# Seven half products in place of eight for the first MoE matrix product, from the third unit on

## The chip, the cores and the metric

The kernel runs on one core of a Trainium2 chip. A core has a matrix engine (PE; its weight loads are shown apart, as PEld), a vector engine (DVE), a scalar engine (ACT), GpSimd (POOL), and SyncE (SP), which here only issues DMAs. The metric is the device time of one execution in microseconds. Three runs of the kernel before gave 729.53 to 730.95 us, with a median of 729.84 us.

## The reference

Local attention with block summaries, and then a two-layer MoE part whose activation is h - tanh(h):

```
k_sum = k.reshape(B, H, nb, 32, D).max(axis=3);  v_sum = v.reshape(B, H, nb, 32, D).mean(axis=3)
scores_l = scale * q @ k^T, kept where |i - j| < 16
scores_s = scale * q @ k_sum^T + log(32)
a = softmax(concat(scores_l, scores_s));  attn = a @ concat(v, v_sum)
x = attn as [3072 tokens, 512]
h = x @ w_in          # 512 -> 2048, the first MoE matrix product
out = (h - tanh(h)) @ w_out
```

B = 4, H = 8, 768 positions, head width 64. Everything is float32. The weights are drawn as float64 numbers, and the kernel turns their words into float32 itself.

## The kernel before

**Units.** The 3072 tokens are cut into eight units of U = 384 tokens (half a batch). For each unit, attention runs head pair by head pair (NP = 4), in slots of the main loop; the MoE part of a unit follows 22 slots later (LAG), one block f of 128 hidden columns per slot, NF = 16 blocks to a unit.

**The first product.** `moe_in(u, f)` makes h transposed: 128 hidden columns by 384 tokens in one PSUM bank (tag pH, two of them). From unit 1 on each float32 operand is split into two float32r parts, high and low, and the product is the sum of high x high, low x high and high x low. With four chunks of 128 along the model width that is 12 matmuls of 384 moving columns, and each of them loads 128 weight columns of its own. The high parts of the weights are `wh`, the low parts are `wl` (they lie in the buffers `wf`), the parts of x are `xh` and `xl`, made by `x_split`. In unit 0 the product runs in full float32 from `wf` and `split_whole` splits the weights on the way.

**The activation and the second product.** `moe_act_small` reads the bank twice (tanh into gt, square into gu) and gu once more, multiplies the two (g, into gv), and `moe_split` splits g into gh and gl. `moe_out(u, f)` then adds three matmuls of 512 columns to each of three banks pY0 to pY2, nine in all for a block. After 16 blocks `store_y` copies the banks out through the buffers `tmp`.

**What sets the order.** All work is first written down as tasks with the buffers that they read and write. `Plan.schedule` then lays them out in one pass with a cost for each kind, and the list that comes out is the program order of every engine and of SP's DMA queue. Ties and priorities go by tables of offsets (BIAS, KB, SL, HALF). A task may have several engines to choose from (`either`). Buffers with one tag form a ring in program order: a new user waits for the last reader of the buffer that it takes over. The ring `wraw` (three buffers of 4 KB per partition) takes the raw weights, later the chunks of k and v from which the block sums of the later batches are made (`sum_chunks`); `tmp` (three) takes weight words, later the output rows.

**Names in the profile.** All instructions are issued through one wrapper, so the profile gives line 68 for each of them; groups are told apart by their tiles. `pH<-xh,wh` is a matmul of the first product, `pY<-wh,gh` one of the second, `pS<-k,q` scores, `pX<-probT,vw` values, `<-ident,...` transposes.

Of the kernel before, what the change touches and what calls it, by code (L numbers as in the profile page):

```python
# [23 lines left out]
RAWB = 3  # L24
# [35 lines left out]
class Engine:  # L60


    def __init__(self, tc, engine):
        self._tc, self._engine = tc, engine

    def __getattr__(self, name):
        op = getattr(self._engine, name)
        return lambda *args, **kwargs: self._tc.keep_in_program_order(op(*args, **kwargs))  # L68
# [7 lines left out]
HELD = {"w shift", "w low", "w sign", "w low part", "w low part 2", "w high part", "w high part 2", "w scale", "normal", "g high", "g low", "g", "cube", "big", "top pre", "sum guard"}  # L76
# [220 lines left out]
def program(  # L297
# [41 lines left out]

    cpool = ctx.enter_context(tc.tile_pool(name="cpool", bufs=1))  # L340
    wk = ctx.enter_context(tc.tile_pool(name="wk", bufs=2))
    pp = ctx.enter_context(tc.tile_pool(name="pp", bufs=1, space=bass.MemoryType.PSUM))

    px_bank = pp.tile([P, 512], F32, name="pX", tag="pX", bufs=1)
    plan = Plan()

    def do(kind, engine, cost, go, r=(), w=()):
        plan.add(kind, {engine: cost}, go, r, w)

    def either(kind, costs, go, r=(), w=()):  # L350
        if len(costs) > 1:
# [34 lines left out]
    def act(n):  # L386
        return 0.12 + n / 1400
# [104 lines left out]
    def convert(i):  # L492
        f = i // 2
        raw, tmp, res = ("raw", i), ("wt", i), ("w", i)
        buf(raw, "wraw", [P, 2 * DM], U32, RAWB)

        def load():
            if i % 2 == 0:
                src = w_in[:, f * P:(f + 1) * P].rearrange("(c p) n -> p c n", p=P)
                sync.dma_start(at(raw).rearrange("p (c n) -> p c n", c=NC), src.bitcast(U32))  # L500
            else:
                sync.dma_start(at(raw), w_out[f * P:(f + 1) * P, :].bitcast(U32))
        dma("w load", load, P * 8 * DM, 1024 if i % 2 == 0 else 4096, w=[(raw, 0), (raw, 1)])
        buf(tmp, "tmp", [P, DM], F32, 3)

        def words():
            x = at(raw).rearrange("p (n two) -> p n two", two=2)
            return x[:, :, 0], x[:, :, 1], at(tmp)

        def scale(e):  # L510

            _, high, w = words()
            copy(e, w, high.bitcast(F32), 2.0 ** -112)

        def shift():
            w = at(tmp).bitcast(U32)
# [47 lines left out]

    top_of = {}
# [544 lines left out]
```

## Time and profile before

| what | value |
|---|---|
| runs | 729.53, 729.84, 730.95 us |
| the profiled execution, its own time | 725.67 us |
| its span, from the first to the last instruction | 723.9 us |
| mean granted TensorE clock | 0.995 |
| busy share of PE, PEld, DVE, ACT, POOL | 97, 81, 35, 61, 40% |
| DMA | 61.02 MB, 84 GB/s over the span |
| start of the last output copy of unit 0 and of unit 7 | 165.0 and 716.6 us |

The profiled execution is 0.6% below the median of the runs; 1.8 us of its time lie around the span. A busy PE isn't PE at its peak, since matmuls overlap and the ends of their rows are modelled; what a matmul costs in a stream is read from the distance of its start from the next one's. A group row gives the count of its instructions, the busy time, the mean of one in ns and the idle time before them. In the chain, the work that ended last is followed back from the end; its pieces in order of time give a start, a length and how many instructions were merged. The last output copy of unit 1 begins at 258.8 us, so the stretch from 258 us on holds the MoE work of units 2 to 7, and attention up to the last unit beside it.

### The profile page before, as it was taken

The page shows a single profiled execution, that of the slowest core. Times are in us where ns is not written, and L with a number is a line of the kernel's source. Part 1 is how long each engine was busy: PE and PEld are TensorE (multiplying, and loading weights), DVE is VectorE, ACT ScalarE, POOL GpSimd, SP SyncE. Part 2 cuts the span into 40 slices and gives each one's busy share as a digit, 9 for nine tenths or more (in the row PEclk, how much of TensorE's full clock was granted, in tenths as well). Part 3 has the DMA queues.
Part 4 walks back from the last instruction along what each step waited for, and adds up shares of the span by engine and source line. Part 5 has one row for each costly group of instructions (what it writes and reads, how often), then busy time and mean ns, then how long its engine had stood idle before and what let it go on. Part 6 is the DMA issues. An engine that isn't in the chain of part 4 may idle for free.

```text
span 723.9 us, 13669 instructions
## 1 busy us (share of the span) xinstructions
PE 702.3 (97%) x4875; PEld 589.4 (81%) x4875; DVE 251.3 (35%) x842; ACT 442.0 (61%) x1341; POOL 289.3 (40%) x391
## 2 busy tenths in 40 slices
PE   5889999999999999999999999999999999999995
PEld 5776555568889889898988889889898898889984
DVE  3459899893322431521322032232222201110000
ACT  4468777767765665666765466557666556545442
POOL 3001223166333463653444447433343524345443
PEclk9999999999999999999999999999999999999998
DMA  8977667734311150241312012113111201000001
GB/s 208 233 205 204 211 209 211 190 114 132 86 44 43 61 149 10 69 105 56 73 37 50 30 44 71 42 38 93 41 45 29 72 30 41 1 30 16 0 1 49
DMA packets 121518, 61.02 MB, mean 84 GB/s; under 512 B 92512, under 2 KB 113248, under 8 KB 121440
## 3 DMA queue, kind: packets, MB, share of 16 engines
q1 hardware_dynamic: 121440, 60.06, 31.2%
q8 instruction: 40, 0.66, 0.4%
q14 instruction: 38, 0.31, 0.1%
HBM read 51.38 MB, written 6.29 MB: 80 GB/s over the span
## 4 chain that ended last, share of the span: by engine, by line
PE 84%; DMA 5%; ACT 3%; SPq 2%; DVE 2%; POOL 2%; issue 1%; POOLq 0%; DVEq 0%
PE pY L68 36%; PE pH L68 35%; PE pS L68 8%; PE pX L68 5%; SPq L68 2%; DMA wraw<-in_moe_w_out_dram 2%; ACT prob L68 1%; DVE tmp L68 1%; POOL wraw L68 1%; DMA wraw<-in_moe_w_in_dram 1%; DMA gl<-in_v_dram 1%; DMA rawk<-in_k_dram 1%; DMA vw<-in_v_dram 1%; DMA vw<-mean 1%; ACT gu L68 1%
## 5 line engine op out<-in xcount | busy, mean ns | idle before, releaser
L68 PE MATMUL pH<-xh,wf 128*128 128x384 f32 x548 | 185.2, 371 | 0.0
L68 POOL TENSOR_TENSOR gl<-gv,gh 128x384 fp32r<-128x384 f32 x110 | 111.7, 1017 | 169.8 <-ACT gh L68 127.4
L68 PE MATMUL pY<-wf,gh 128*128 128x512 f32 x432 | 177.9, 440 | 0.0
L68 PE MATMUL pH<-xh,wh 128*128 128x384 f32 x448 | 152.9, 341 | 0.0
L68 PE MATMUL pH<-xl,wh 128*128 128x384 f32 x448 | 150.8, 337 | 0.0
L68 PE MATMUL pY<-wh,gh 128*128 128x512 f32 x336 | 140.0, 417 | 0.0
L68 ACT ACTIVATE gu<-pH 128x384 f32<-128x384 f32 x128 | 62.7, 490 | 120.3 <-PE pH L68 94.6
L68 PE MATMUL pY<-wh,gl 128*128 128x512 f32 x336 | 132.3, 394 | 0.0
L68 POOL TENSOR_TENSOR gv<-gu,gt 128x384 f32<-128x384 f32 x95 | 97.3, 1024 | 86.2 <-ACT gu L68 55.3
L68 PEld LDWEIGHTS pH<-xh,wf 128*128 128x128 f32 x548 | 102.5, 188 | 21.4 <-issue 2.8
L68 ACT ACTIVATE prob<-prob,stat 128x118 f32<-128x118 f32 x246 | 91.8, 384 | 22.3 <-DVE stat L68 22.0
L68 PEld LDWEIGHTS pY<-wf,gh 128*128 128x128 f32 x432 | 80.5, 189 | 23.5 <-issue 12.1
L68 DVE CUSTOM_DVE_ANT_0 prob<-pS,mask 128x118 f32<-128x118 f32 x180 | 41.1, 275 | 149.3 <-PE pS L68 125.6
L68 PEld LDWEIGHTS pH<-xh,wh 128*128 128x128 f32 x448 | 84.2, 188 | 3.9 <-issue 0.6
L68 PEld LDWEIGHTS pH<-xl,wh 128*128 128x128 f32 x448 | 84.0, 188 | 0.0
L68 PEld LDWEIGHTS pY<-wh,gl 128*128 128x128 f32 x336 | 63.2, 188 | 14.9
L68 PEld LDWEIGHTS pY<-wh,gh 128*128 128x128 f32 x336 | 63.3, 188 | 11.7 <-issue 2.6
L68 ACT ACTIVATE gh<-gv 128x384 fp32r<-128x384 f32 x82 | 43.1, 525 | 44.5 <-PE pY L68 37.0
L68 ACT ACTIVATE gu<-gu 128x384 f32<-128x384 f32 x128 | 66.9, 523 | 0.0
L68 ACT ACTIVATE gt<-pH 128x384 f32<-128x384 f32 x128 | 61.8, 483 | 0.1
L68 DVE CAST gh<-gv 128x384 fp32r<-128x384 f32 x30 | 11.1, 370 | 135.8 <-PE pY L68 107.7
L68 PE MATMUL pS<-k,q 128*64 128x118 f32 x720 | 42.3, 267 | 0.3 <-ACT k L68 0.3
(130 smaller groups left out, 814.2 us busy)
## 6 DMA issues: line engine op xcount, KB each, us to landing
wraw<-in_moe_w_in_dram SPq DMA_DIRECT2D x16, 512.0 KB
wraw<-in_moe_w_out_dram SPq DMA_DIRECT2D x16, 512.0 KB
rawq<-in_q_dram SPq DMA_DIRECT2D x48, 128.0 KB
out_dram<-tmp SPq DMA_DIRECT2D x24, 256.0 KB
rawk<-in_k_dram SPq DMA_DIRECT2D x32, 128.0 KB
vw<-in_v_dram SPq DMA_DIRECT2D x40, 96.0 KB
vw<-in_v_dram SPq DMA_DIRECT2D x48, 64.0 KB
wraw<-in_k_dram SPq DMA_DIRECT2D x16, 192.0 KB
```

Source lines behind the costliest of these rows:

```text
L68: return lambda *args, **kwargs: self._tc.keep_in_program_order(op(*args, **kwargs))
```

## The change

From unit 2 on, two blocks of hidden columns, g and g + 8, are made together (`moe_in_seven`, g = 0 to 7). The product of the two blocks (256 hidden columns) with the unit (512 by 384) is taken as a two by two product of halves: halves of the model width (256) and halves of the tokens (UH = 192). In place of its eight half products seven are made, with sums of quarters of the operands (the scheme of Strassen and Winograd).

- A half product is 6 matmuls (two chunks, three parts) of 192 moving columns, so a pair has 42 matmuls of 192 columns where it had 24 of 384.
- The four sums of weight quarters are made once, in unit 1, from the split weights (`make_sums`), split into high and low again, and stored to device memory: 16 stores of 512 KB. For each pair they come back in two loads of 512 KB into `wraw` (`load_sums`), 96 loads in all.
- x of a unit is kept whole (`x whole`) and `x_operands` makes four differences of its quarters (8 instructions of 192 columns), and the high and low parts of seven operands.
- The seven products accumulate in two banks of pH, z and y. z is read out four times and y three (`part` and `join`, 192 columns each), through a buffer `s3` into gu. tanh and square then read gu in SBUF, not the bank.
- Room is made for this: `tmp` has two buffers (three before), gu three (two before), the chunks of k and v go through `tmp`, q and k of attention have one buffer from unit 2 on (two before), and the operands of x have one each. The first halves of the weights of blocks 8 to 15 (`wa`) are given up after unit 1.
- In `split_whole` the weights of blocks 8 to 15 are split in two halves each. The tables of the planner are replaced, and so the order of the tasks changes everywhere.

The diff, without the tables and the second program for large values:

```diff
...
-    if not small_only:
+    if small_only:
+        RINGS |= {"gu": 3}
+    else:
         RINGS |= {"gt": 1, "gq": 1}
+    TMPS = 2 if small_only else 3
+    FH, UH, DH = NF // 2, U // 2, DM // 2
+    def seven(u):
+        return small_only and u >= 2
+    def in_halves(i):
+        return small_only and i % 2 == 0 and i // 2 >= FH
...
-            fixed(("wh", i), [P, DM], F32R)
+            if in_halves(i):
+                buf(("wa", i), f"wa{i // 2 - FH}", [P, DH], F32R)
+                fixed(("wb", i), [P, DH], F32R)
+            else:
+                fixed(("wh", i), [P, DM], F32R)
...
-        buf(tmp, "tmp", [P, DM], F32, 3)
+        buf(tmp, "tmp", [P, DM], F32, TMPS)
...
+        x, low = ("wf", i), buf(("wl", i), f"wf{n - 1}" if n else "wl", [P, DM], F32R)
+        parts = [(0, ("wa", i), slice(0, DH)), (1, ("wb", i), slice(DH, DM))] if in_halves(i) else [(0, ("wh", i), slice(0, DM))]
+        for k, high, cs in parts:
+            m = cs.stop - cs.start
+            either("w high part 2", {ACT: act(m) + 0.04, DVE: dve(m, True)}, lambda e, high=high, cs=cs: copy(e, at(high), at(x)[:, cs]), r=[(x, 0)], w=[(high, 0)])
+            do("w low part 2", DVE, dve(m), lambda high=high, cs=cs: vector.tensor_tensor(at(low)[:, cs], at(x)[:, cs], at(high).bitcast(F32), op=ALU.subtract), r=[(x, 0), (high, 0)], w=[(low, k)])
...
+    def w_high(i, c):
+        if in_halves(i):
+            return at(("wb" if c >= NC // 2 else "wa", i))[:, P * (c % (NC // 2)):P * (c % (NC // 2) + 1)]
+        return w_parts(i)[0][:, P * c:P * (c + 1)]
...
+    SCR = ("scr",)
+    if small_only:
+        spool = ctx.enter_context(tc.tile_pool(name="spool", bufs=1, space=bass.MemoryType.DRAM))
+        made[SCR] = spool.tile([FH, 2, P, 4 * DH], F32, name="scr")
+    def make_sums(g):
+        ia, ib = 2 * g, 2 * (g + FH)
+        t0, t1, sf = buf(("tw", g, 0), "tmp", [P, DM], F32, TMPS), buf(("tw", g, 1), "tmp", [P, DM], F32, TMPS), buf(("sf", g), "wraw", [P, 4, DH], F32, RAWB)
+        def add(kind, n, out, x, y, op, r, w):
+            either(kind, {DVE: dve(n), POOL: pool(n)}, lambda e: e.tensor_tensor(out(), x(), y(), op=op), r=r, w=w)
+        add("s whole", DM, lambda: at(t0), lambda: w_parts(ia)[0].bitcast(F32), lambda: w_parts(ia)[1].bitcast(F32), ALU.add, w_keys(ia), [(t0, 0)])
+        for k, n in enumerate(("wa", "wb")):
+            cs = slice(DH * k, DH * (k + 1))
+            add("s whole", DH, lambda cs=cs: at(t1)[:, cs], lambda n=n: at((n, ib)).bitcast(F32), lambda cs=cs: at(("wl", ib))[:, cs].bitcast(F32), ALU.add, [((n, ib), 0), (("wl", ib), k)], [(t1, k)])
+        a11, a12, a21, a22 = (lambda t=t, k=k: at(t)[:, DH * k:DH * (k + 1)] for t in (t0, t1) for k in range(2))
+        s1, s2, s3, s4 = (lambda n=n: at(sf)[:, n] for n in range(4))
+        add("s mix", DH, s1, a21, a22, ALU.add, [(t1, 0), (t1, 1)], [(sf, 0)])
+        add("s mix", DH, s2, s1, a11, ALU.subtract, [(sf, 0), (t0, 0)], [(sf, 1)])
+        add("s mix", DH, s3, a11, a21, ALU.subtract, [(t0, 0), (t1, 0)], [(sf, 2)])
+        add("s mix", DH, s4, a12, s2, ALU.subtract, [(t0, 0), (sf, 1)], [(sf, 3)])
+        for h in range(2):
+            st = buf(("so", g, h), "wraw", [P, 2, 2, DH], F32R, RAWB)
+            keys = [(sf, 2 * h), (sf, 2 * h + 1)]
+            either("s high", {ACT: act(DM), DVE: dve(DM, True)}, lambda e, st=st, h=h: copy(e, at(st)[:, :, 0], at(sf)[:, 2 * h:2 * h + 2]), r=keys, w=[(st, 0)])
+            either("s low", {DVE: dve(DM), POOL: pool(DM)}, lambda e, st=st, h=h: e.tensor_tensor(at(st)[:, :, 1], at(sf)[:, 2 * h:2 * h + 2], at(st)[:, :, 0].bitcast(F32), op=ALU.subtract), r=keys + [(st, 0)], w=[(st, 1)])
+            dma("s store", lambda st=st, h=h: sync.dma_start(made[SCR][g, h], at(st).rearrange("p a b c -> p (a b c)").bitcast(F32)), P * 16 * DH, 4096, r=[(st, 0), (st, 1)], w=[(SCR, (g, h))])
+    def load_sums(u, g, h):
+        st = buf(("sx", u, g, h), "wraw", [P, 2, 2, DH], F32R, RAWB)
+        dma("s load", lambda: sync.dma_start(at(st).rearrange("p a b c -> p (a b c)").bitcast(F32), made[SCR][g, h]), P * 16 * DH, 4096, r=[(SCR, (g, h))], w=[(st, 0)])
...
-            st = buf(("ch", which, b, g, c), "wraw", [P, 8, D], F32, RAWB)
+            st = buf(("ch", which, b, g, c), "tmp", [P, 8, D], F32, TMPS) if small_only else buf(("ch", which, b, g, c), "wraw", [P, 8, D], F32, RAWB)
...
+    def qk_of(u, p):
+        return 0 if seven(u) else p % 2
...
-        qf, kf = ("qf", p % 2), ("kf", p % 2)
+        qf, kf = ("qf", qk_of(u, p)), ("kf", qk_of(u, p))
...
+        if u == 0 and WHOLE_IN or seven(u):
+            if not small_only:
+                buf(("xf", u, p), f"xh{p}", [P, U], F32, 2)
+            elif p == 0:
+                buf(("xf", u), "xf", [P, NC, U])
+            key = (("xf", u), p) if small_only else (("xf", u, p), 0)
+            either("x whole", {ACT: 0.371, DVE: 0.465}, lambda e: copy(e, x_whole(u, p), at(px)[:, :U]), r=[(px, i) for i in range(NT)], w=[key])
...
+        if small_only:
+            buf(xh, f"o{p}", [P, U], F32R)
+            buf(xl, f"o{NC + p}", [P, U], F32R)
...
+    def x_operands(u):
+        xf, tags = ("xf", u), iter(range(12))
+        def part(c, h):
+            return at(xf)[:, c, UH * h:UH * (h + 1)]
+        T = {}
+        for n in range(4):
+            for j in range(2):
+                T[n, j] = buf(("T", u, n, j), f"wa{2 * n + j}", [P, UH])
+        mixes = [(0, lambda j: part(j, 1), lambda j: part(j, 0), lambda j: [(xf, j)]),
+                 (1, lambda j: part(2 + j, 1), lambda j: at(T[0, j]), lambda j: [(xf, 2 + j), (T[0, j], 0)]),
+                 (2, lambda j: part(2 + j, 1), lambda j: part(j, 1), lambda j: [(xf, 2 + j), (xf, j)]),
+                 (3, lambda j: part(2 + j, 0), lambda j: at(T[1, j]), lambda j: [(xf, 2 + j), (T[1, j], 0)])]
+        for n, x, y, keys in mixes:
+            for j in range(2):
+                either("x mix", {DVE: dve(UH), POOL: pool(UH)}, lambda e, n=n, j=j, x=x, y=y: e.tensor_tensor(at(T[n, j]), x(j), y(j), op=ALU.subtract), r=keys(j), w=[(T[n, j], 0)])
+        for name in ("B11", "B21", "T2", "T1", "T3", "T4", "B22"):
+            high, low = (name, u, 0), (name, u, 1)
+            if name == "B22":
+                both = buf((name, u), "q1", [P, 2, 2, UH], F32R)
+                made_by[high], made_by[low] = lambda: at(both)[:, 0], lambda: at(both)[:, 1]
+                hk, lk = (both, "h"), (both, "l")
+            else:
+                for x in (high, low):
+                    buf(x, f"o{next(tags)}", [P, 2, UH], F32R)
+                hk, lk = (high, "h"), (low, "l")
+            if name[0] == "B":
+                c, h = 2 * (name[1] == "2"), int(name[2]) - 1
+                src = [(lambda c=c, h=h: at(xf)[:, c:c + 2, UH * h:UH * (h + 1)], slice(0, 2), [(xf, c), (xf, c + 1)], 2 * UH)]
+            else:
+                src = [(lambda t=T[int(name[1]) - 1, j]: at(t), j, [(T[int(name[1]) - 1, j], 0)], UH) for j in range(2)]
+            for k, (x, cs, keys, n) in enumerate(src):
+                hkk, lkk = [(hk[0], hk[1] + str(k))], [(lk[0], lk[1] + str(k))]
+                either("x high", {ACT: act(n), DVE: dve(n, True)}, lambda e, x=x, cs=cs, high=high: copy(e, at(high)[:, cs], x()), r=keys, w=hkk)
+                either("x low", {DVE: dve(n), POOL: pool(n)}, lambda e, x=x, cs=cs, high=high, low=low: e.tensor_tensor(at(low)[:, cs], x(), at(high)[:, cs].bitcast(F32), op=ALU.subtract), r=keys + hkk, w=lkk)
+            x_keys[u, name] = [(b, n + str(k)) for b, n in (hk, lk) for k in range(len(src))]
+    x_keys = {}
+    def moe_in_seven(u, g):
+        z, y = bank(("z", u, g), "pH"), bank(("yx", u, g), "pH")
+        ha, hb = (buf(("gu", u, f), "gu", [P, U], F32, RINGS["gu"]) for f in (g, g + FH))
+        if ("s3",) not in made_by:
+            buf(("s3",), "k1", [P, 3, UH])
+        s3, ia, ib = ("s3",), 2 * g, 2 * (g + FH)
+        def of_w(i, c0):
+            return lambda c: (w_high(i, c0 + c), w_low(i, c0 + c)), [(("wb", i), 0), (("wl", i), 1)] if in_halves(i) else w_keys(i)
+        def of_s(n):
+            st = ("sx", u, g, n // 2)
+            return lambda c: tuple(at(st)[:, n % 2, k, P * c:P * (c + 1)] for k in range(2)), [(st, 0)]
+        def product(w, x, ps, start):
+            w, keys = w
+            def go():
+                o = at(ps)[:, :UH]
+                for c in range(2):
+                    high, low = w(c)
+                    xh, xl = at((x, u, 0))[:, c], at((x, u, 1))[:, c]
+                    tensor.matmul(o, high, xh, start=start and c == 0, stop=False, skip_group_check=not start)
+                    tensor.matmul(o, low, xh, start=False, stop=False, skip_group_check=not start)
+                    tensor.matmul(o, high, xl, start=False, stop=c == 1, skip_group_check=not start)
+            do("in", PE, 0.53, go, r=keys + x_keys[u, x], w=[(ps, 0)])
+        def part(out, key):
+            either("part", {ACT: 0.27, DVE: 0.28}, lambda e: copy(e, out(), at(z)[:, :UH]), r=[(z, 0)], w=[key])
+        def join(out, key, n):
+            do("join", DVE, 0.28, lambda: vector.tensor_tensor(out(), at(y)[:, :UH], at(s3)[:, n], op=ALU.add), r=[(y, 0), (s3, n)], w=[key])
+        product(of_w(ia, 0), "B11", z, True)
+        product(of_w(ia, 2), "B21", y, True)
+        part(lambda: at(s3)[:, 0], (s3, 0))
+        join(lambda: at(ha)[:, :UH], (ha, 0), 0)
+        product(of_s(1), "T2", z, False)
+        part(lambda: at(s3)[:, 1], (s3, 1))
+        product(of_s(0), "T1", y, True)
+        product(of_s(2), "T3", z, False)
+        part(lambda: at(s3)[:, 2], (s3, 2))
+        join(lambda: at(hb)[:, UH:], (hb, 1), 2)
+        product(of_w(ib, 2), "T4", z, False)
+        part(lambda: at(hb)[:, :UH], (hb, 0))
+        product(of_s(3), "B22", y, False)
+        join(lambda: at(ha)[:, UH:], (ha, 1), 1)
...
+        t, sq = buf(("gt", u, f), "gt", [P, U], F32, RINGS["gt"]), ("gu", u, f)
+        if seven(u):
+            h, hk, sk = (lambda: at(sq)), [], [(sq, 0), (sq, 1)]
+        else:
+            buf(sq, "gu", [P, U], F32, RINGS["gu"])
+            h, hk, sk = (lambda: at(("ph", u, f))[:, :U]), [(("ph", u, f), 0)], [(sq, 0)]
         n = NF * u + f
-        do("tanh", ACT, 0.37, lambda: scalar.activation(at(t), at(ph)[:, :U], AF.Tanh, scale=EC), r=[(ph, 0)], w=[(t, 0)])
-        do("square", ACT, 0.47, lambda: scalar.activation(at(sq), at(ph)[:, :U], AF.Square, accum_out=sums_seen[:, n:n + 1]), r=[(ph, 0)], w=[(sq, 0), (SEEN, n)])
-        do("series", ACT, 0.42, lambda: scalar.activation(at(sq), at(sq), AF.Tanh, scale=EA), w=[(sq, 0)])
+        do("tanh", ACT, 0.37, lambda: scalar.activation(at(t), h(), AF.Tanh, scale=EC), r=hk or sk, w=[(t, 0)])
+        do("square", ACT, 0.47, lambda: scalar.activation(at(sq), h(), AF.Square, accum_out=sums_seen[:, n:n + 1]), r=hk, w=sk + [(SEEN, n)])
+        do("series", ACT, 0.42, lambda: scalar.activation(at(sq), at(sq), AF.Tanh, scale=EA), w=sk)
...
+        u, n = divmod(m, NF)
+        return u, n // 2 + FH * (n % 2) if seven(u) else n
...
-            moe_in(*m)
+            if not seven(m[0]):
+                moe_in(*m)
+            elif m[1] < FH:
+                if m[1] == 0:
+                    x_operands(m[0])
+                for h in range(2):
+                    load_sums(*m, h)
+                moe_in_seven(*m)
             moe_act(*m)
+            if small_only and m[0] == 1 and m[1] >= FH:
+                make_sums(m[1] - FH)
...
```

More of the change, by code (lines that the diff above doesn't have):

```diff
@@ L46 @@
-HALF = {'const': (12, 12), 'k load': (29, 38), 'top pre': (16, 16), 'q load': (9, 15), 'top turn': (8, 8), 'q turn': (4, 9), 'top max': (8, 8), 'q high': (8, 18), 'v load': (44, 63), 'k turn': (5, 9), 'k high': (5, 9), 'top put': (6, 11), 'scores': (4, 9), 'min': (24, 54), 'exp': (24, 54), 'sum': (8, 8), 'sum out': (7, 8), 'sum guard': (4, 9), 'inverse': (4, 9), 'normal': (24, 54), 'p turn': (12, 24), 'p out': (12, 24), 'mean turn': (2, 4), 'mean out': (2, 4), 'mean put': (6, 10), 'values': (4, 4), 'w load': (8, 32), 'x whole': (4, 4), 'w scale': (6, 32), 'w shift': (6, 32), 'w low': (6, 32), 'w sign': (6, 32), 'w high part 2': (6, 32), 'w low part 2': (3, 32), 'in': (2, 20), 'square': (2, 19), 'tanh': (2, 19), 'series': (2, 19), 'g': (1, 19), 'out': (1, 51), 'x high': (0, 4), 'x low': (0, 4), 'chunk load': (0, 11), 'chunk max': (0, 4), 'chunk sum': (0, 4), 'y out': (0, 3), 'y store': (0, 3), 'g high': (0, 2), 'g low': (0, 2), 'top high': (0, 0), 'seen': (0, 0), 'seen turn': (0, 0), 'seen max': (0, 0), 'w high part': (3, 26), 'w low part': (3, 26), 'w sign 1': (4, 12), 'w sign 2': (4, 12), 'top low': (1, 2), 'cube': (2, 18), 'big': (2, 17), 'direct': (2, 17), 'pick': (2, 17), 'q low': (0, 2), 'q again': (0, 2), 'k low': (0, 2), 'k again': (0, 2)}
@@ new lines @@
+HALF = {'const': (12, 12), 'k load': (29, 38), 'q load': (9, 15), 'top pre': (16, 16), 'v load': (44, 63), 'top turn': (8, 8), 'top max': (8, 8), 'q turn': (5, 9), 'q high': (10, 18), 'k turn': (5, 9), 'k high': (5, 9), 'top put': (7, 10), 'scores': (5, 9), 'min': (30, 54), 'exp': (30, 54), 'sum': (8, 8), 'sum out': (8, 8), 'sum guard': (5, 9), 'inverse': (5, 9), 'normal': (30, 54), 'p turn': (15, 24), 'p out': (12, 24), 'mean turn': (2, 4), 'mean out': (2, 4), 'mean put': (6, 10), 'values': (4, 4), 'x whole': (4, 4), 'w load': (7, 32), 'w scale': (6, 32), 'w shift': (4, 32), 'w low': (4, 32), 'w sign': (4, 32), 'w high part 2': (4, 40), 'w low part 2': (2, 35), 'in': (2, 18), 'square': (2, 17), 'tanh': (2, 17), 'series': (2, 17), 'g': (2, 16), 'out': (3, 41), 'x high': (0, 4), 'x low': (0, 4), 'g high': (0, 0), 'g low': (0, 0), 'y out': (0, 0), 'y store': (0, 0), 's whole': (0, 0), 's mix': (0, 0), 's high': (0, 0), 's low': (0, 0), 's store': (0, 0), 'chunk load': (0, 0), 'chunk max': (0, 0), 'x mix': (0, 0), 'chunk sum': (0, 0), 'part': (0, 0), 'join': (0, 0), 's load': (0, 0), 'top high': (0, 0), 'seen': (0, 0), 'seen turn': (0, 0), 'seen max': (0, 0), 'w high part': (3, 26), 'w low part': (3, 26), 'w sign 1': (4, 12), 'w sign 2': (4, 12), 'top low': (1, 2), 'cube': (2, 18), 'big': (2, 17), 'direct': (2, 17), 'pick': (2, 17), 'q low': (0, 2), 'q again': (0, 2), 'k low': (0, 2), 'k again': (0, 2)}
@@ L794, in scores_and_values @@
             banks = [bank(("s", u, p, n), tag) for n, tag in enumerate(tags)]
-            r, w, cost = r + score_keys(p), w + [(x, n) for x in banks for n in range(4)], cost + 1.23
+            r, w, cost = r + score_keys(u, p), w + [(x, n) for x in banks for n in range(4)], cost + 1.23
             parts.append(lambda: score(*now))
@@ L842, in transpose_probs, with x_whole @@
         either("p out", {ACT: 0.28, DVE: 0.335}, lambda e: copy(e, at(pt)[:N2], at(t)[:N2, :2 * P].rearrange("p (a f r) -> p a f r", a=2, f=2)), r=[(t, 0)], w=[(pt, 0)])
+    def x_whole(u, c):
+        return at(("xf", u))[:, c] if small_only else at(("xf", u, c))
     def x_split(u, p):
         px = ("px", u, p)
-        if u == 0 and WHOLE_IN:
-            xf = buf(("xf", u), "xh", [P, NC, U], F32, 2) if p == 0 else ("xf", u)
-            either("x whole", {ACT: 0.371, DVE: 0.465}, lambda e: copy(e, at(xf)[:, p], at(px)[:, :U]), r=[(px, i) for i in range(NT)], w=[(xf, p)])
-            return
@@ new lines, in x_split @@
+        xh, xl = ("xh", u, p), ("xl", u, p)
+        if small_only:
+            buf(xh, f"o{p}", [P, U], F32R)
+            buf(xl, f"o{NC + p}", [P, U], F32R)
+        else:
+            buf(xh, f"xh{p}", [P, U], F32R, 2)
+            buf(xl, f"xl{p}", [P, U], F32R, 2)
+        either("x high", {ACT: 0.371, DVE: 0.465}, lambda e: copy(e, at(xh), at(px)[:, :U]), r=[(px, i) for i in range(NT)], w=[(xh, 0)])
+        do("x low", DVE, 0.47, lambda: vector.tensor_tensor(at(xl), at(px)[:, :U], at(xh).bitcast(F32), op=ALU.subtract),
+           r=[(px, i) for i in range(NT)] + [(xh, 0)], w=[(xl, 0)])
@@ L863, in go @@
                 for c in range(NC):
[L864 to L865 removed]
+                    tensor.matmul(at(ph)[:, :U], at(("wf", i))[:, P * c:P * (c + 1)], x_whole(u, c), start=c == 0, stop=c == NC - 1)
+            do("in", PE, 2.65, go, r=[(("wf", i), 0)] + [(("xf", u), c) if small_only else (("xf", u, c), 0) for c in range(NC)], w=[(ph, 0)])
             split_whole(i)
```

59 lines of the change are left out of this document (27 added, 32 removed).

## The prediction, made blind

> **What bounds the kernel now.** I read the page first: the busy shares, the clock, and the chain of work that ended last.
>
> ```profile
> PE 702.3 (97%) x4875; PEld 589.4 (81%) x4875; DVE 251.3 (35%) x842; ACT 442.0 (61%) x1341; POOL 289.3 (40%) x391
> ...
> PEclk9999999999999999999999999999999999999998
> ...
> PE 84%; DMA 5%; ACT 3%; SPq 2%; DVE 2%; POOL 2%; issue 1%; POOLq 0%; DVEq 0%
> ```
>
> The chain is 84% PE at an open clock, and nothing else holds more than 5%. The busy times by stretch (before unit 1's MoE work, during it, and after it, where the change acts) show how much room there is.
>
> ```profile
> core 0: us, PE busy (x) PEld busy (x) DVE busy (x) ACT busy (x) POOL busy (x), PEclk, DMA share, GB/s
> 0.00:165.00 165.00, 150.74 (x1095) 99.36 (x1096) 125.60 (x343) 107.33 (x318) 40.97 (x76) 0.99 0.72 198
> 165.00:258.00 93.00, 93.00 (x729) 83.17 (x728) 30.77 (x125) 62.02 (x202) 40.39 (x59) 1.00 0.28 72
> 258.00:724.00 466.00, 458.54 (x3055) 406.88 (x3053) 94.94 (x374) 272.63 (x823) 207.90 (x258) 1.00 0.18 46
> ```
>
> In the last stretch PE is never idle until the end, DVE is busy a fifth of the time, ACT 59%, POOL 45%, DMA 18%. The waits of the weight loads there are small: of 13 groups, these are the first three.
>
> ```profile
> PEld pX L68 <- issue: 4.2, 14, 0.4
> PEld pY L68 <- issue: 2.0, 13, 0.2
> PEld pX L68 <- ACT k L68: 0.7, 2, 0.4
> ```
>
> They add up to less than 12 us of 466. So the time from unit 2 on is PE's instruction stream, and the change is priced by what its matmuls cost there. Pieces of the chain in order of time give that price without the modelled ends:
>
> ```profile
> 648.40 4.16 PE pH L68 x24
> 653.27 4.17 PE pH L68 x24
> ...
> 705.38 11.18 PE pY L68 x48
> ```
>
> 24 matmuls of the first product, exactly a pair of blocks, take 4.17 us, 0.174 us each; 48 of the second, with 512 columns, take 0.233 us each. Both are 0.453 to 0.455 ns per column, so these streams are bound by the moving columns. With 192 columns that rate gives 0.087 us, and 42 of them 3.65 us.
>
> **The change, part by part.** *The seven products.* Each of the 42 matmuls still brings 128 weight columns of its own, and now has half the columns to hide the load behind. So the question is what a load costs. Its rows by shape:
>
> ```profile
> L68 PEld LDWEIGHTS pH<-xh,wh 128*128 128x128 f32 x448 | 84.2, 188 | 3.9 <-issue 0.6 <-ACT xh L68 0.3
> L68 PEld LDWEIGHTS pY<-k,q 128*64 128x64 f32 x48 | 2.4, 137 | 0.4 <-POOL k L68 0.3
> L68 PEld LDWEIGHTS pS<-vacc,ident 96*24 96x24 f32 x32 | 1.8, 102 | 1.4 <-ACT th L68 0.7 <-ACT gu L68 0.4 <-ACT k L68 0.4
> L68 PEld LDWEIGHTS pS<-ident,stat 128*1 128x1 f32 x1 | 0.1, 82 | 0.1
> ```
>
> A load of 1, 24, 64 and 128 columns takes 82, 102, 137 and 188 ns: a fixed latency, which may overlap, and (188 - 82) / 127 = 0.835 ns per column, so 0.107 us for 128. That those 0.107 us can't be shared with another load is seen where PE starts from idle on the first product, loads and matmuls by start:
>
> ```profile
> 499.83 0.19 PEld L68 LDWEIGHTS pH<-xh,wh 128*128 128x128 f32 x1 [0.15 <-ACT xh L68]
> 499.94 0.19 PEld L68 LDWEIGHTS pH<-xh,wf 128*128 128x128 f32 x1
> 500.12 0.19 PEld L68 LDWEIGHTS pH<-xl,wh 128*128 128x128 f32 x1
> 500.29 0.19 PEld L68 LDWEIGHTS pH<-xh,wh 128*128 128x128 f32 x1
> ```
> ```profile
> 499.83 0.44 PE L68 MATMUL pH<-xh,wh 128*128 128x384 f32 x1
> 500.11 0.34 PE L68 MATMUL pH<-xh,wf 128*128 128x384 f32 x1
> 500.29 0.34 PE L68 MATMUL pH<-xl,wh 128*128 128x384 f32 x1
> ```
>
> In the stream a load starts with the matmul before its own (500.11 and 500.12, then 500.29 and 500.29): one set of weights ahead, no more. The first load found an empty array, and yet the second could start only 0.11 us later, when the first matmul had taken its weights over; that first matmul shows 0.44 in place of 0.34 us for the same reason. So a step of the stream is the longer of the matmul's columns and the next load. With 384 columns that is the columns (0.174); with 192 it is the load, 0.11 against 0.087.
>
> A stream of loads behind very short matmuls exists too, 12 columns behind 64-column loads (24 of them, two column halves side by side, so twelve steps):
>
> ```profile
> 13.23 0.84 PEld L68 LDWEIGHTS pY<-blk,gu 128*64 128x64 f32 x24
> 13.33 0.84 PE L68 MATMUL pY<-blk,gu 128*64 128x12 f32 x24
> ```
>
> (0.84 - 0.14) / 11.5 is 0.061 us per 64 columns, so such a stream is bound by loads, at up to 0.122 us when doubled to 128. The ends for a step are thus 0.087 (load hidden after all) and 0.122, with 0.107 from the slope between; I take 0.110, because 499.83 to 499.94 is the same weights, type and shape. A pair of blocks then takes 42 x 0.110 = 4.62 us in place of 4.17, 0.45 us more. There are 8 pairs in each of 6 units, 48 in all: **+21.6 us**. The ends: +15.6 at 0.107 (42 x 0.107 - 4.17 = 0.324 us a pair), +45.8 at 0.122, -24.8 at 0.087.
>
> *Reading out.* Four `part` and three `join` of 192 columns a pair, where tanh and square read the bank directly. The nearest rows:
>
> ```profile
> L68 ACT ACTIVATE probT<-pS 118x256 f32<-118x256 f32 x59 | 20.0, 385 | 7.9 <-PE pS L68 7.6
> L68 DVE TENSOR_TENSOR gt<-gt 128x192 f32<-128x192 f32 x6 | 2.1, 358 | 5.0 <-DMA gt<-in_k_dram 5.0
> L68 DVE TENSOR_TENSOR xl<-pX,xh 128x384 fp32r<-128x384 f32 x28 | 15.4, 551 | 10.6 <-ACT xh L68 10.4
> ```
>
> At 0.385 and 0.358 us, a unit adds 32 x 0.385 = 12 us to ACT and 24 x 0.358 = 9 us to DVE. `x_operands` adds 16 instructions of 192 columns on DVE or POOL (16 x 0.358 = 6 us), three lows of 384 (3 x 0.551) and 11 highs on ACT (about 4 us); it takes away four `x low` (2 us). ACT goes from 273 / 6 = 45 to about 61 us per unit, DVE from 16 to about 31, in a unit of 78 to 81 us. Both stay beneath PE, so the cost is nothing so long as PE has other work. It is a new wait on PE, though: T2, T3 and T4 go into z and must wait for the `part` before, and behind the waiting product stand all later matmuls, whose results ACT, DVE and POOL wait for. The cover is the 18 matmuls of 0.233 us that the same pair owes the second product, 4.2 us, and attention. Without it one such wait costs the pipe's tail (0.34 - 0.17 us, the shown length less the step) and a read of 0.385, 0.55 us.
>
> *Attention with one buffer for q and k.* The next head pair's copies wait for the scores of the last, 24 times. Cover: the same stream; 1 to 2 us each if it is gone. I take nothing.
>
> *Sums through device memory.* 96 loads of 512 KB on SP. A landing of that size in the chain, and the rate of the dense start:
>
> ```profile
> 112.69 5.11 DMA wraw<-in_moe_w_out_dram
> ...
> GB/s 208 233 205 204 211 209 211 190 114 132 86 44 43 61 149 10 69 105 56 73 37 50 30 44 71 42 38 93 41 45 29 72 30 41 1 30 16 0 1 49
> ```
>
> At 208 GB/s 16 loads are 8.4 MB and 40 us of a unit's 80, on queues that are 18% busy. With three buffers, two of which a pair holds, one load goes a whole pair (10 us) ahead, and the other from T1 of the pair before to T3, about as long; 5.11 us fit in. A load that waits for its buffer stands on SP ahead of the q, k, v loads and the output stores; a wait of a few us there costs nothing while those are early. Not hidden, a late load would cost up to 5 us once.
>
> *Making the sums*, in unit 1: per pair about 0.73 + 6 x 0.4 + 2 x 0.73 = 4.6 us, mostly on DVE, from this row and half of it (192 columns took 0.358):
>
> ```profile
> L68 DVE TENSOR_TENSOR wf<-wf,wh 128x512 fp32r<-128x512 f32 x31 | 22.7, 732 | 0.5
> ```
>
> That is 37 us beside 31 in a stretch of 93: hidden, but `wraw` and `tmp` are held in turn by stores of 5 us and by chunk loads, and unit 2's operands need the last `wa` free. I take **+2 us** for this handover and for the end, where both blocks of the last pair come out together; ends 0 and +10.
>
> *The start.* `tmp` with two buffers, `wh` in halves, a new order. PE isn't the bound before 165 us (DMA 72%, DVE 126 of 165), so it could move either way; no row prices it. I take 0, with -5 to +6. The waits of PE that are left in the last stretch could fall by up to 12; I take 0, because PE's partners get more to do.
>
> Sum: 21.6 + 2 = +23.6 us. From the profiled execution, 725.67 us, that is 749.3; this one lies 4.2 us below the median shown, 729.84, and I keep that distance: 753.4, **753.5 us**.
>
> **The rivals.** *A, the load hides:* a step of 0.087, 3.65 us a pair, and 729.8 - 24.8 = **705 us**. For it speaks that in every stream seen, loads of 0.107 us were hidden behind the columns; against it the 0.11 at 499.83. It decides below a step of 4.17 / 42 = 0.099 us. The Trainium skill (TensorE: Matmul & The Clock Gate, Back-to-back issue gap) gives about 81 ns for a sustained load and matmul pair at 128 columns; by that 42 steps would be at least 3.4 us, an estimate on this rival's side. Its section on weight-path perf modes has a fast load for 128 weight columns whose type isn't FP32; the row of 188 ns, which lies on the slope of the float32 loads, shows none here.
>
> *B, the read-outs show on PE:* the forecast and one uncovered wait of 0.55 us a pair on top, 48 x 0.55 = 26 us, **780 us**. For it: two banks only, a chain of four z steps; against it: PE gets slower by 0.45 us a pair, which lets its partners come earlier.
>
> *C, it comes out even:* the step near 0.099, or fewer waits and a shorter start eating a step of 0.107 (15.6 - 12 - 5), **729 us**.
>
> **How the numbers follow.** Load-bound with the waits covered 0.66; B 0.15; A 0.14; C 0.05. The range takes in 0.107 with all that could fall (729.8 + 15.6 - 10 = 735) and B with a little more: 736 to 783. A is left outside. A change under 0.2% (1.5 us) can't be told from none here: faster 0.15, the same 0.04, slower 0.81.
>
> **What would show it.** Right: 2016 matmuls of 192 columns, six in a row in the chain 0.66 us long, loads still 188 ns, PEld busier than 90% within the first product, PE full from 258 us on, unit 1 ending where it did. Wrong: six in 0.52 us (A); PE idle before pH by ACT or DVE (B); waits on DMA `wraw` from device memory; or a later end of unit 1.

## The result, and the profile after

The changed kernel is slower. Four runs of it gave a median of 763.77 us (761.51 to 766.03), four of the kernel before on the same chip 730.39 us (729.53 to 731.22): a ratio of 1.0457, with a 95% interval of 1.0421 to 1.0493, or 33.4 us. The profiled execution of after took 764.61 us, 762.9 of them its span.

The page of after: busy times, the granted clock, and the bytes moved.

```profile
PE 734.8 (96%) x5747; PEld 619.3 (81%) x5747; DVE 396.7 (52%) x1188; ACT 517.3 (68%) x1569; POOL 296.4 (39%) x413
...
PEclk9958999999999999999999999999999999999998
...
DMA packets 137660, 119.93 MB, mean 157 GB/s; under 512 B 94304, under 2 KB 115040, under 8 KB 137568
```

PE is busy as before, with more and shorter matmuls; DVE goes from 35 to 52%, and the bytes from 61.02 to 119.93 MB. By stretch (start and end, length, busy time and instructions of PE, PEld, DVE, ACT and POOL, clock, DMA share, GB/s), cut at 165 us as for the kernel before, and at 262 us, where the last output copy of unit 1 lies (261.9):

```profile
0.00:165.00 165.00, 149.64 (x1067) 97.89 (x1068) 116.78 (x332) 104.14 (x311) 33.62 (x77) 0.94 0.70 187
165.00:262.00 97.00, 93.78 (x690) 80.82 (x689) 72.73 (x184) 73.64 (x228) 44.19 (x58) 1.00 0.55 173
262.00:750.00 488.00, 486.63 (x3975) 437.34 (x3976) 207.22 (x673) 337.23 (x1028) 216.76 (x277) 1.00 0.50 146
```

From 262 us on PE is full for 486.6 of 488 us: little starves it (its weight loads wait 13.6 us there, all groups together, and 11.2 in the kernel before), but its stream has become longer. The weight loads of the first product in a stretch of that stream, by their starts:

```profile
500.38 0.87 PEld L68 LDWEIGHTS pH<-o,wraw 128*128 128x128 f32 x6
501.18 0.19 PEld L68 LDWEIGHTS pH<-o,wh 128*128 128x128 f32 x1
501.29 0.19 PEld L68 LDWEIGHTS pH<-o,wf 128*128 128x128 f32 x1
501.40 0.30 PEld L68 LDWEIGHTS pH<-o,wh 128*128 128x128 f32 x2
501.62 0.19 PEld L68 LDWEIGHTS pH<-o,wf 128*128 128x128 f32 x1
501.73 0.19 PEld L68 LDWEIGHTS pH<-o,wh 128*128 128x128 f32 x1
```

From 501.18 to 501.73 there are five steps in 0.55 us. Over the whole kernel the middle half of the steps is 0.111 to 0.112 us. A pair of blocks is then 42 x 0.112 = 4.70 us in place of 4.17, and 48 pairs make **+25.6 us** of the 33.4. The other 8 are sought in the experiments.

### The profile page after: what moved, and what is told of

The parts are those of the page before. It is cut to its first block, busy times and chain, and to the rows that moved or that the text cites. A ratio compares the mean times of both kernels' runs of the same rounds, so it can differ in the third digit from the quotient of the medians.

```text
span 762.9 us, 16442 instructions
## 1 busy us (share of the span) xinstructions
PE 734.8 (96%) x5747; PEld 619.3 (81%) x5747; DVE 396.7 (52%) x1188; ACT 517.3 (68%) x1569; POOL 296.4 (39%) x413
## 2 busy tenths in 40 slices
DMA packets 137660, 119.93 MB, mean 157 GB/s; under 512 B 94304, under 2 KB 115040, under 8 KB 137568
## 5 line engine op out<-in xcount | busy, mean ns | idle before, releaser
L68 DVE TENSOR_TENSOR gu<-pH,k 128x192 f32<-128x192 f32 x144 | 51.3, 356 | 166.0 <-PE pH L68 93.2
L68 PEld LDWEIGHTS pH<-o,wraw 128*128 128x128 f32 x864 | 109.7, 191 | 12.5 <-DMA wraw<-scr 2.2
L68 PE MATMUL pH<-o,wraw 128*128 128x192 f32 x864 | 114.8, 275 | 2.8 <-DMA wraw<-scr 2.8
L68 ACT ACTIVATE gu<-gu 128x384 f32<-128x384 f32 x224 | 112.3, 514 | 0.9
L68 PE MATMUL pH<-o,wh 128*128 128x192 f32 (+1 forms) x448 | 94.2, 284 | 0.7 <-DVE o L68 0.7
L68 PE MATMUL pH<-o,wf 128*128 128x192 f32 (+1 forms) x324 | 92.9, 287 | 0.0
L68 PEld LDWEIGHTS pH<-o,wh 128*128 128x128 f32 x448 | 75.5, 191 | 4.7 <-DVE gu L68 0.8
L68 ACT ACTIVATE gt<-gu 128x384 f32<-128x384 f32 x96 | 47.2, 516 | 26.1 <-DVE gu L68 25.8
L68 PEld LDWEIGHTS pH<-o,wf 128*128 128x128 f32 x324 | 61.6, 190 | 2.3
L68 PE MATMUL pH<-o,wb 128*128 128x192 f32 (+1 forms) x224 | 49.5, 283 | 0.0
```

## The experiments

All are compared with runs of the kernel before, made beside them on the same chip; its medians there were 728.4 us (experiments 1 to 4), 729.7 (5 to 8) and 729.7 (9 to 11). The planner lays the work out anew whenever a task, a cost or a buffer changes. Experiments 3 to 8 have such an order of their own; 2 and 9 to 11 issue after's program in after's order, 1 before's in before's.

### 1. The kernel before, with its first product cut in two

Nothing of the seven products is in it: from unit 2 on each matmul of 384 columns becomes two of 192 with the same weights.

```diff
-                tensor.matmul(o, high[:, c], at(xh)[:, c], ...)
-                tensor.matmul(o, low[:, c], at(xh)[:, c], ...)
-                tensor.matmul(o, high[:, c], at(xl)[:, c], ...)
+                for w, x, n in ((high, xh, 0), (low, xh, 1), (high, xl, 2)):
+                    for h in ((slice(0, U // 2), slice(U // 2, U)) if u >= 2 else (slice(0, U),)):
+                        tensor.matmul(o[:, h], w[:, c], at(x)[:, c, h], ...)
```

> The kernel before, in its own order, with each matmul of the first product from unit 2 on cut into two of 192 columns with the same weights: 48 in place of 24 for a pair of blocks, nothing else changed. Load-bound theory (a step is the longer of the columns, 0.087 us, and the next weight load, 0.112 as the changed kernel's trace shows): 48 x 0.112 = 5.38 us in place of 4.17 a pair, 48 pairs, +58 us, about 788 us. Rival: the 0.112 belongs to the changed kernel's operands (sums that arrive by DMA, new buffers), not to the load; then 48 x 0.087 = 4.18, no change, 730 us.

One run took 784.18 us, 55.8 more. The trace has the loads of each pair twice, though the weights are the same (weight loads of this kernel, in order of time):

```profile
500.70 0.30 PEld L68 LDWEIGHTS pH<-xh,wf 128*128 128x128 f32 x2
500.92 0.30 PEld L68 LDWEIGHTS pH<-xl,wh 128*128 128x128 f32 x2
501.14 0.30 PEld L68 LDWEIGHTS pH<-xh,wh 128*128 128x128 f32 x2
501.37 0.30 PEld L68 LDWEIGHTS pH<-xh,wf 128*128 128x128 f32 x2
```

Two steps take 0.22 us, where one of 384 columns took 0.174. 48 steps of 0.112 in place of 4.17 us make 1.21 us a pair, 58 in all: the size of the matmul alone gives the price, without sums, read-outs or a new order.

### 2. 240 columns in place of 192 in half of the matmuls

If the columns set the step, 48 more of them in 1008 of the 2016 matmuls cost 48 x 0.453 ns x 1008 = 22 us; if the load does, nothing. The further columns land in a part of the bank that nobody reads.

```diff
+                    if c == 0:
+                        o, xh, xl = (at(ps)[:, :240], *(at((x, u, k)).rearrange("p c n -> p (c n)")[:, :240] for k in range(2)))
...
```

> The changed kernel, with 240 moving columns in place of 192 in half of its 2016 matmuls (the first chunk of each product; the 48 extra columns are written to PSUM and read by nobody). Load-bound theory: 240 columns take 0.109 us, still less than the load's 0.112, so nothing changes, 764 us within 3. Rival: a step is the columns plus a fixed 0.025 us for each matmul; then 1008 x 0.022 = +22 us, 786 us.

764.3 us (ratio 1.0471, 1.0417 to 1.0524), where after has 763.8 (1.0457). A quarter more columns in half of the matmuls cost nothing that can be told. The weight loads of one half product of this kernel, the first three for matmuls of 240 columns, the last three of 192:

```profile
501.51 0.19 PEld L68 LDWEIGHTS pH<-o,wh 128*128 128x128 f32 x1
501.62 0.19 PEld L68 LDWEIGHTS pH<-o,wf 128*128 128x128 f32 x1
501.73 0.30 PEld L68 LDWEIGHTS pH<-o,wh 128*128 128x128 f32 x2
501.96 0.19 PEld L68 LDWEIGHTS pH<-o,wf 128*128 128x128 f32 x1
502.07 0.19 PEld L68 LDWEIGHTS pH<-o,wh 128*128 128x128 f32 x1
```

The step is 0.11 for both lengths. The Trainium skill (TensorE: Matmul & The Clock Gate, LDWEIGHTS) gives a load 1/1.2 ns per column, by which 128 would take an estimated 107 ns; the 112 ns measured here lie 5 above it. The Trainium skill's about 81 ns for a sustained pair of load and matmul (TensorE: Matmul & The Clock Gate, Back-to-back issue gap) is for 128 moving columns, which no first product here has; at 192 and 240 the steps stay at 0.11 us. The transposes of before, which do move 128 columns (`pS<-ident,rawk`), follow each other at 0.108 us (median), so this trace doesn't show the 81.

### 3. Fewer loads: high times both parts of x in one matmul

`xh` and `xl` lie side by side, so that high x [xh | xl] is one matmul of 384 columns into both halves of the bank, and low x xh one of 192: four loads where there were six. The read-out has to add the two halves, on DVE.

```diff
-                    tensor.matmul(o, high, xh, ...)
-                    tensor.matmul(o, low, xh, ...)
-                    tensor.matmul(o, high, xl, ...)
+                    tensor.matmul(o, high, at((x, u))[:, :, c], ...)
+                    tensor.matmul(o[:, 1], low, at((x, u, 0))[:, c], ...)
...
-            either("part", {ACT: 0.27, DVE: 0.28}, lambda e: copy(e, out(), at(z)[:, :UH]), ...)
+            do("part", DVE, 0.47, lambda: vector.tensor_reduce(out(), at(z)[:, :U].rearrange("p (k n) -> p n k", k=2), ...), ...)
```

> The changed kernel, with the two matmuls that use the same high weights joined into one of 384 columns (high and low part of x side by side, into two halves of the bank), so that a product is 2 x (384 + 192) columns behind 4 loads in place of 6 x 192 behind 6; the halves are added when they are read out, on DVE (part as a reduction of 384 elements, join as two additions). Load-bound theory: 14 x (0.174 + 0.112) = 4.00 us a pair in place of 4.70, -34 us, 730 us, unless DVE's 10 instructions a pair show. Fixed cost of 0.025 us a matmul: 14 x (0.199 + 0.112) = 4.35, -17 us, 747 us.

780.8 us (1.0754, 1.0664 to 1.0844), slower than after. The steps shrank about as expected: a load follows the one before it by 0.177 us behind a matmul of 384 columns and by 0.108 behind one of 192 (medians). But PE's busy time from 262 us on (the second number of the stretch) falls 27 us short of its length, and the read-outs of z on DVE now took 0.55 us each:

```profile
262.00:725.00 463.00, 435.55 (x3122) 377.86 (x3121) 310.59 (x869) 292.00 (x884) 193.14 (x257) 0.99 0.51 150
```

The order was redrawn as well, so this run doesn't say which of the two was dear.

### 4. No sums, order redrawn

The products with sums take plain weights, and neither making, storing nor loading of sums is left (so the output isn't the reference's).

```diff
-            st = ("sx", u, g, n // 2)
-            return lambda c: tuple(at(st)[:, n % 2, k, P * c:P * (c + 1)] for k in range(2)), [(st, 0)]
+            c0 = 2 * (n % 2)
+            return lambda c: (w_high(ia, c0 + c), w_low(ia, c0 + c)), w_keys(ia)
...
-                for h in range(2):
-                    load_sums(*m, h)
...
-            if small_only and m[0] == 1 and m[1] >= FH:
-                make_sums(m[1] - FH)
```

> The changed kernel without the weight sums: none are made, stored or loaded, and the four products that use them take quarters of the plain weights (so h is not the product; the bound that starts the second program is raised for that). PE's work is the same 2016 steps. Of the 33 us that the change costs, 48 x (42 x 0.112 - 4.17) = 26 us are the steps. If the other 7 are the handover from unit 1 to 2, where unit 2 waits for the last sums: 757 us. If they are the start and the end: 764 us.

761.2 us (1.0446, 1.0396 to 1.0496): 2.6 us below after by the medians, with an order of its own. The interval overlaps that of after, so this run alone doesn't show that the sums cost anything. Experiment 11, the same without a new order, comes out 6 us lower.

### 5 and 6. What the planner's tables and costs do

After with the tables of before, and after with the cost of a half product that the trace shows (6 x 0.112 = 0.672 in place of 0.53).

```diff
-BIAS = {('const', 0): -2330.5, ...}
+BIAS = {('const', 1): 103, ...}
...
```
```diff
-            do("in", PE, 0.53, go, r=keys + x_keys[u, x], w=[(ps, 0)])
+            do("in", PE, 0.672, go, r=keys + x_keys[u, x], w=[(ps, 0)])
```

> The changed kernel with the four tables of the kernel before, so with another order of the same work. The steps are the same 2016 at 0.112 us. If the new order is what costs the rest beyond the 26 us of the steps (the first two units end about 10 us behind in work done), the old tables give most of it back: about 757 us. If the rest is the work itself, 764 us or, with tables that don't fit it, more.

> The changed kernel, planned with 0.672 us (6 x 0.112) for a half product in place of 0.53. Load-bound theory: PE has no more than about 10 us of waits from 262 us on, so a better order can't win more: 758 to 764 us. Rival: the order, planned for products that are too short, is what costs: under 750 us.

789.2 us (1.083, 1.0776 to 1.0885) and 772.8 us (1.0605, 1.0552 to 1.0658). The same work in another order cost 25 and 9 us more, the second with a truer cost in the planner. So what an experiment with a redrawn order shows is the edit and an order together; 9 to 11 keep the order.

### 7 and 9. The joint matmuls, one half of the bank read

As 3, but `part` and `join` stay as in after and read the half of high x xh alone; the small corrections in the other half are left out of the result. In 7 the order is redrawn, in 9 every engine's program is after's. What 9 changes of after is the two kinds of step, and the corrections that nobody reads.

```diff
-                    tensor.matmul(o, high, xh, ...)
-                    tensor.matmul(o, low, xh, ...)
-                    tensor.matmul(o, high, xl, ...)
+                    tensor.matmul(o, high, at(pair_of[x, u])[:, :, c], ...)
+                    tensor.matmul(o[:, 1], low, at((x, u, 0))[:, c], ...)
```

> The joined matmuls of e3_joint_parts, read out as in the changed kernel (one half of the bank alone: what high x low and low x high add is left out of h). 4 loads a product in place of 6: 14 x (0.171 + 0.108) = 3.91 us a pair in place of 4.70, as the steps in e3's trace show, -38 us: 726 us. If e3 lost its gain to the joined matmuls themselves and not to its longer read-outs, about 780 us again.

> As e7_joint_one_half (joined matmuls, one half of the bank read, what high x low and low x high add left out of h), but each engine's program in exactly the changed kernel's order: e7's and e3's orders were drawn up anew. PE's work is 48 x (4.70 - 3.91) = 38 us less. If PE's stream alone sets the end, 726 us. If the chain of read-outs behind the two banks and ACT's and DVE's part of a pair come next, the gain stops at what they allow; from e7's 759 us, where PE was idle 22 us and slower in its steps, that would be 735 to 755 us. If e7's order was the reason, near 726.

759.2 us (1.0405, 1.0353 to 1.0457) with the redrawn order, and **733.7 us** (1.0046, 1.0016 to 1.0076) in after's. Weight loads of 9:

```profile
500.45 0.19 PEld L68 LDWEIGHTS pH<-op,wb 128*128 128x128 f32 x1
500.56 0.19 PEld L68 LDWEIGHTS pH<-op,wf 128*128 128x128 f32 x1
500.74 0.19 PEld L68 LDWEIGHTS pH<-op,wb 128*128 128x128 f32 x1
500.85 0.19 PEld L68 LDWEIGHTS pH<-op,wf 128*128 128x128 f32 x1
501.03 0.19 PEld L68 LDWEIGHTS pY<-wh,gh 128*128 128x128 f32 x1
```

Two steps, 0.11 and 0.18, do the work of three. The columns are the same as in after; the number of loads went from 42 to 28 a pair, and 30 us went with it. By the steps of 3 it should be 48 x (42 x 0.112 - 14 x (0.177 + 0.108)) = 34 us (the expectation had 38, with 0.171 for the longer step). The weight loads of 9 wait 20.7 us from 262 to 750 us, all groups together, and those of after 13.6, which is more than the 4 that are missing; they weren't separated further. The two runs also price an order once more: 7 and 9 issue the same work, 25 us apart.

### 8. Before with two buffers of tmp

```diff
-        buf(tmp, "tmp", [P, DM], F32, 3)
+        buf(tmp, "tmp", [P, DM], F32, 2)
...
```

> The kernel before with two tmp buffers in place of three, nothing else. If this ring holds the weight conversions of the start up, 3 to 4 us slower, 732 us; if not, the same 728 to 729 us.

732.6 us (1.004, 1.0013 to 1.0067), 2.9 more, with an order redrawn by the smaller ring. That is the price of the lost buffer and of the new order together; nothing here separates the two.

### 10. The joint matmuls with the whole read-out, in after's order

The full product again, as in 3, but in after's order: a `part` on DVE is a reduction of 384 elements, one on ACT a copy with a DVE addition behind it, and a `join` is two additions.

```diff
+                    copy(e, out(), at(z)[:, :UH])
+                    vector.tensor_tensor(out(), at(z)[:, UH:U], out(), op=ALU.add)
...
+                vector.tensor_tensor(out(), at(y)[:, :UH], at(s3)[:, n], op=ALU.add)
+                vector.tensor_tensor(out(), at(y)[:, UH:U], out(), op=ALU.add)
```

> As e3_joint_parts, with the whole read-outs (384 elements on DVE for a part, or ACT with an addition on DVE behind it; two additions for a join), in the changed kernel's order. It computes the full product. If longer read-outs show on PE through the chain of z: slower than e9 by about 7 x 0.25 = 1.8 us a pair at most, 48 pairs, so up to 86 us where nothing covers them; e3 against e7 was 22 us. I expect 745 to 775 us, and under 729 only if PE's stream alone sets the end.

782.9 us (1.074, 1.0708 to 1.0772): 49 us more than 9, whose matmuls it shares, and above the 745 to 775 that were expected. The waits of the weight loads from 262 to 750 us (waited for: us in total, times, longest), first of this kernel:

```profile
PEld pH L68 <- DVE k L68: 32.9, 54, 2.1
PEld pH L68 <- DVE gu L68: 22.1, 50, 1.8
PEld pH L68 <- issue: 3.8, 10, 1.0
```

And of after, in the same stretch:

```profile
PEld pH L68 <- DVE gu L68: 3.0, 14, 0.3
PEld pH L68 <- issue: 1.9, 4, 1.5
PEld pH L68 <- DVE k L68: 1.5, 8, 0.3
```

So rival B's mechanism is real: when a read-out takes two instructions, or one over 384 elements, PE's weight loads wait 55 us for z and y. With one short instruction they wait 4.5 in after. DVE as a whole is far from full in 10 all the while (297 of 488 us, the third busy time):

```profile
262.00:750.00 488.00, 463.72 (x3161) 385.95 (x3162) 296.67 (x935) 322.44 (x991) 205.65 (x266) 0.99 0.48 143
```

### 11. No sums, in after's order

As 4, but the instructions that make, store and load the sums are only struck from after's programs.

```diff
-        dma("s load", lambda: sync.dma_start(at(st)..., made[SCR][g, h]), ...)
+        dma("s load", lambda: None, ...)
```

> As e4_no_sums (no sums made, stored or loaded, plain weights in their place, h not the product), in the changed kernel's order. What this takes off is what the sums cost: their instructions on DVE and ACT in unit 1, 59 MB of DMA, and the waits for them. If the 7 us beside the steps are the handover: 757 us. If they are the start and the end: 763 us.

**755.4 us** (1.0352, 1.0324 to 1.0381), 8.4 below after (by the two ratios 0.0105 x 730 = 7.7; their intervals don't meet). By stretch:

```profile
165.00:262.00 97.00, 97.00 (x767) 86.12 (x766) 32.51 (x124) 71.92 (x230) 43.21 (x61) 1.00 0.29 76
262.00:740.00 478.00, 478.00 (x3884) 429.79 (x3882) 202.68 (x659) 330.90 (x1007) 213.44 (x273) 1.00 0.18 46
```

PE has 767 matmuls behind it in the stretch from 165 to 262 us, 77 more than after, and DVE 32.5 us of work in place of 72.7. The waits of the weight loads in unit 1 that after has from 165 to 264 us, and this kernel has not:

```profile
PEld pH L68 <- DMA wraw<-scr: 2.2, 1, 2.2
PEld pY L68 <- POOL gl L68: 1.7, 4, 0.7
...
PEld pH L68 <- DVE o L68: 0.8, 1, 0.8
...
PEld pX L68 <- POOL prob L68: 0.6, 1, 0.6
```

The longest is the first load of sums. The tile of the sums in device memory, of after (duration of an issue, first and last start):

```profile
L68 SPq DMA_DIRECT2D wraw<-scr x96: 319/330/1180, 251.5 to 728.8; - x96
L68 SPq DMA_DIRECT2D scr<-wraw x16: 319/339/778, 177.9 to 251.9; - x16
```

The first load goes out at 251.5, 0.4 us before the last store, and PE begins with the sums when it has landed:

```profile
257.65 0.92 PE L68 MATMUL pH<-o,wraw 128*128 128x192 f32 x6 [1.73 <-DMA wraw<-scr]
```

A load of sums is late once more, the second one of unit 2's third pair:

```profile
278.69 0.89 PE L68 MATMUL pH<-o,wraw 128*128 128x192 f32 x6 [1.07 <-DMA wraw<-scr]
```

Since both kernels issue the same matmuls in the same order, each can be compared with itself. The last output copy of a unit begins at (us):

| unit | after | experiment 11 | later by |
|---|---|---|---|
| 0 | 169.2 | 168.2 | 1.0 |
| 1 | 261.9 | 255.6 | 6.3 |
| 2 | 359.1 | 351.2 | 7.9 |
| 7 | 756.7 | 748.8 | 7.9 |

The first 1.0 isn't the sums': their first instruction starts on DVE at 170.9 us. The rest builds up until 281 us, with the two largest steps at the late loads (1.9 us at 257.65 and 1.2 at 278.69), and from there on nothing is added: all later loads are free. So the sums cost 6.9 us in these two executions, 7.7 by the ratios and 8.4 by the medians, all of it at the handover. Whether the buffers of `wraw`, held by the stores, or the place of the loads in the order kept them back wasn't tried.

The account is then 25.6 (steps) + 7 to 8.4 (sums) = 33 to 34 us, where 33.4 were measured. Without the sums the kernel is 25.7 above its runs of before, which is the steps alone.

## Why the prediction was right, and where it was off

**The bound.** Right. PE is full from 262 us on, and but for one late load of sums (1.2 us) what the change costs there is what its matmuls cost.

**The step of the seven products.** Right in its mechanism: the longer of the columns and the next load. There are 2016 matmuls of 192 columns (by tile 864 + 384 + 264 + 288 + 192 + 24), and their loads still show 0.19 us. The chain of after breaks off at the last copy, so that six in a row can't be read there; the starts of the loads stand for it. The row at 499.83 gave 0.110, and the step is 0.112. That is 48 x 42 x 0.002 = 4 us of the distance: +25.6 in place of +21.6. Experiments 1, 2 and 9 show the cause from three sides: the same weights loaded twice, longer matmuls for nothing, fewer loads with the same columns.

One reading on the way to it doesn't hold. The straight line through the loads of 1, 24, 64 and 128 columns leaves out rows of the same view of before, loads for transposes:

```profile
L68 PEld LDWEIGHTS pS<-ident,prob 128*118 128x118 f32 x120 | 14.7, 136 | 6.2 <-POOL prob L68 1.9 <-issue 1.5 <-PE pS L68 0.3
L68 PEld LDWEIGHTS pS<-ident,rawk 128*128 128x128 f32 x112 | 13.3, 140 | 3.1 <-ACT probT L68 0.6 <-issue 0.6
```

They show 136 and 140 ns for 118 and 128 columns, hardly more than the 137 for 64. So the length of a load's row doesn't give the price of its columns, nor does it tell a fast load from a plain one; that the 0.107 from the slope came close is luck, as far as these rows show. What carried the forecast was the distance of two starts, 0.11 at 499.83.

**Read-outs at nothing.** Right, though with less room than the argument said. They were priced well: `part` on ACT and `join` on DVE were taken at 0.385 and 0.358 us, and the page of after has

```profile
L68 ACT ACTIVATE k<-pH 128x192 f32<-128x192 f32 (+1 forms) x107 | 35.9, 335 | 46.5 <-PE pH L68 45.5
L68 DVE TENSOR_TENSOR gu<-pH,k 128x192 f32<-128x192 f32 x144 | 51.3, 356 | 166.0 <-PE pH L68 93.2
```

ACT and DVE are busy 337 / 6 = 56 and 207 / 6 = 35 us a unit (61 and 31 predicted). But busy shares of this kind are no cover by themselves: in experiment 10 DVE had 191 of 488 us to spare, and the weight loads waited 55 for it. What covered the read-outs was that each came before PE needed the bank.

**One buffer for q and k; 96 loads on SP.** Right from the fourth pair of unit 2 on: after 281 us the loads that are left add nothing (experiment 11), and no wait for q or k is among the large ones. The two late loads, in the first and the third pair, belong to the handover.

**Making the sums and the handover.** This is the mis-sized term: +2 us was taken, with ends of 0 and +10, and experiment 11 has 7 to 8.4. The work was sized well, 37 us on DVE against 72.7 - 32.5 = 40 measured. The step that failed is to call 37 us beside 31 in a stretch of 93 hidden: DVE had room over the stretch, but PE waited in it for results that came late one by one (POOL `gl` 1.7 us, DVE `o` 0.8, POOL `prob` 0.6), and unit 2's first sums had to go to device memory and back before PE could use them. The forecast named the stores and the buffers of this handover, and gave them too little. Its two signs are both there: waits on `wraw` from device memory, and a later end of unit 1 (261.9 us, and 255.6 in the same order without the sums).

**The start at nothing.** The last copy of unit 0 begins at 169.2 in place of 165.0 us. But it begins at 168.2, 167.0 and 164.7 in experiments 11, 9 and 10, which have after's order, and at 167.8 in experiment 1, which has before's program there. So the start moves by about as much between executions as it does here, and nothing of it shows as the change's. Without the sums the whole kernel lies 25.7 above before, so the start and the rest of the edits cost nothing in the sum; a gain and a loss that cancel aren't excluded.

**The rivals.** A, the load hides, falls by experiments 1 and 2; C with it. B doesn't occur in the change (4.5 us of such waits, where it was given 26), and does in experiment 10. The predicted 753.5 us is 10.3 below the time: 4 by the step, 5 to 6 by the sums, and 0.6 because before itself had 730.4 in place of 729.8.

**A version that beats both** didn't come out of this: 9 comes within 0.5% of before, and leaves the corrections out.

## What to carry to other kernels

Before a product is cut into fewer but smaller ones, price a matmul at the longer of its moving columns and its weight load: here a matmul gets no cheaper below 0.112 / 0.000453 = about 247 columns. By the same steps, 42 matmuls of 0.112 us cost less than 24 of twice the columns only if the halves have more than 42 x 0.112 / (48 x 0.000453) = about 216 columns, an estimate without read-outs and sums; these had 192. Where loads are the bound, fewer loads help more than fewer columns, so long as the read-out doesn't grow with it. And where a planner sets the order, compare variants in one fixed order: redrawn ones moved the time here by 6 to 25 us with the same work, as much as the edits that were to be priced.

## What the runs showed of the hardware that was not expected

- A load isn't skipped when the next matmul has the same weights: experiment 1 shows both, at steps of 0.112 us, and is 55.8 us slower.
- In before, the rows of loads of 128 columns are 188 ns long in the two products and 140 ns for transposes, and yet the next load can follow as soon in both: at 0.108 us for the transposes, at 0.112 for the first product in after.
- The granted clock dips early in after (the 5 in the third slice of its row, 0.94 over the first 165 us), which it doesn't in the profile of before (0.99). The profile of experiment 1, whose first two units are before's, has the dip too (a 7 in that slice), so the sums and the new order aren't what makes it; what does stays open.
